# Attention of two heads on 64 rows of TensorE each, and the first gating units of batch 0 among the pairs of batch 1

## The chip, the cores and the metric

The program runs on one core of a Trainium2 chip. The metric is the device time of one execution in microseconds (us), lower is better. The kernel before took 448.5 us (median of three runs, 447.94 to 448.64). Beside these runs one execution was recorded by the hardware profiler: its own time is 448.29 us, and its trace spans 446.5 us from the first to the last instruction.

The engines that matter: TensorE (PE in the profile, with its weight loads as PEld), VectorE (DVE), ScalarE (ACT), GpSimd (POOL), and SyncE (SP), which issues the DMAs. Each works through its own instructions in order.

## The reference

```python
# attention: 2 batches, 12 heads, 448 positions, 64 dimensions per head
scores = cap * tanh((q @ k.T / 8) / cap)
attn = exp(scores - max); attn = attn / (sum(attn) + 1e-9)
x = attn @ v                              # heads side by side: (2, 448, 768)
# gated block
h = gelu_tanh(x @ w_in)                   # 768 -> 1024, halves u and v of 512
v_n = (v - mean(v)) / sqrt(var(v) + 1e-6) * g_ln
v_s = w_sg @ v_n + b_sg                   # over the 448 positions
x = x + (u * v_s) @ w_out
# mixer
u = x + (relu(x.T @ w_tok1) @ w_tok2).T   # over positions, 448 -> 256 -> 448
out = u + relu(u @ w_ch1) @ w_ch2         # 768 -> 1536 -> 768
```

All arithmetic is in 32-bit floats. The weights (all but `w_sg`) arrive as 64-bit floats.

## The kernel before

Everything is kept in a product form that TensorE runs at one pass: a float `a` is split into `a(0)`, its rounding to the type `fp32r`, and `a(1)`, the rest, and a product is the sum of three, `a(0)b(0) + a(0)b(1) + a(1)b(0)` (`three`). So each tile that TensorE reads has a cast (`cast`, on ACT, DVE or POOL) and a subtraction (`rest`, on DVE or POOL). Only the product of the attention weights with v is done in plain fp32: its matmul counts as two records in the trace and four passes in time.

**Attention** goes by 12 pairs of heads, six per batch (`attention(n)`). The scores are computed transposed, keys on the 128 output rows, the 448 queries as columns. A head has only 64 dimensions, so the kernel fills the 128 rows of the array with a trick: the tile `K` holds a head's keys on one half of the rows and their rests on the other, and q is loaded twice, once for each half. One matmul then gives two of the products, and two matmuls (with the cast of q and with its rest) give one block of 128 keys. The 448 keys are three blocks of 128 and 64 left over; the left-over keys of both heads share one block of four matmuls. A pair so has 16 matmuls for scores (L270 `sc<-a,K`), 12 records in fp32 for the values (L592 `gm<-a,V`) and 4 matmuls for the left-over keys' values (L604 `gm<-a,R`). ACT takes tanh (L551) and exp (L559) of the scores, two blocks at a time (128x896) with one block (128x448) at the end. Columns of ones beside v give the sums; DVE transposes them (L622), adds the guard, takes reciprocals (L630, L631), spreads them (L636), multiplies (L646) and splits x (L359 or L358, L375).

**After attention**: three v units and then, after a unit for the positions left over from both batches, four u units per batch (`v_unit`: 18 matmuls of 512 columns; `u_unit`: 18 of 448; both with gelu on ACT, L745), then `sg_unit`, `out_unit`, `tr_unit`, `tok1_unit`, `tok2_unit`, `ch1_unit`, `ch2_unit`.

**Weights** (`weight`) are turned from 64-bit to 32-bit on the chip: three ACT instructions (L405, L414, L427) and one of DVE (L434), and then split.

**Order.** Nothing loops: all operations are collected with a key (a due time) and `Plan.schedule` puts them in order by assumed durations, choosing among allowed engines (`ON`, `W_ON`) and giving out buffers from pools (`BUFS`). `gm` has four PSUM banks and `sc` two double ones. The order on each engine is then fixed in the program. Which weights are due when stands in `KEYS`. In the kernel before, the batches' units stand in the order

```python
        for b in range(B):
            vn[b] = stage([lambda s=s: self.v_unit(x[b], win_v, s) for s in range(NR)], 4)
...
        for b in range(B):
            u[b] = stage([lambda f=f: self.u_unit(x[b], win_u, f) for f in range(NF)], 3.4)
```

with keys that all lie after the last pair.

## Time and profile before

| | us |
|---|---|
| median of three runs | 448.5 |
| the profiled execution | 448.29 |
| its span | 446.5 |
| PE busy in the span | 426.6 (96%) |
| PEld busy | 363.9 (82%) |
| DVE busy | 295.0 (66%) |
| ACT busy | 254.8 (57%) |
| POOL busy | 116.6 (26%) |

A share is an average over two very different parts: the attention, to about 124 us, and all that follows. [...]

### The profile page before, as it was taken

Reading aid. Unit: us, or ns where it says so; the run is one execution under the profiler, and the core shown is the slowest. Engines: PE = TensorE matmul, PEld = TensorE weight load, DVE = VectorE, ACT = ScalarE, POOL = GpSimd, SP = SyncE. Lnnn points to the kernel's source line nnn. Section 1 sums busy time; section 2 is a strip of 40 time slices with the busy share of each in tenths; the row PEclk is TensorE's granted clock in tenths of the full one; section 3 lists DMA queues with packets and bytes.
Section 4 is the critical chain, followed back from the end, with each engine's and each line's share of the span. In section 5 each row is a group of like instructions: output and inputs, shape, how many; then the busy total and the mean of one; then the engine's idle time right before and its main releaser. Section 6 shows DMA issues by size and latency. Waiting matters only on the chain.

```text
span 446.5 us, 5466 instructions
## 1 busy us (share of the span) xinstructions
PE 426.6 (96%) x1966; PEld 363.9 (82%) x1966; DVE 295.0 (66%) x483; ACT 254.8 (57%) x380; POOL 116.6 (26%) x133
## 2 busy tenths in 40 slices
PE   8988999988999999999999999999999999999994
PEld 6655675655578899999999988999999999999994
DVE  5999999999998893787337899545454332434220
ACT  6969999988767656632226770755455523444100
POOL 2334566633213440176000177000002010111000
PEclk9999999999999999999999999999999999999998
DMA  7932443522123524402001312433344314452101
GB/s 204 340 116 85 133 147 115 155 65 66 47 94 96 181 83 150 131 0 94 2 0 42 101 48 69 139 123 94 99 137 117 120 37 167 132 159 93 73 37 32
DMA packets 24627, 46.02 MB, mean 103 GB/s; under 512 B 11536, under 2 KB 14352, under 8 KB 24592
## 3 DMA queue, kind: packets, MB, share of 16 engines
q1 hardware_dynamic: 24448, 45.48, 33.0%
q8 instruction: 17, 0.28, 0.3%
q14 instruction: 18, 0.15, 0.1%
q10 hardware_dynamic: 144, 0.11, 0.1%
HBM read 42.83 MB, written 2.75 MB: 102 GB/s over the span
## 4 chain that ended last, share of the span: by engine, by line
PE 70%; DVE 25%; issue 2%; SPq 1%; DMA 1%; DVEq 0%
PE gm L270 48%; PE sc L270 19%; DVE a L375 5%; DVE x L375 4%; DVE h L646 3%; DVE h L622 3%; DVE K L375 2%; DVE h L636 2%; DVE R L359 1%; DVE t L434 1%; PE sc L882 1%; DVE K L359 1%; DVE sm L630 1%; PE gm L592 1%; DVE x L359 1%
## 5 line engine op out<-in xcount | busy, mean ns | idle before, releaser
L270 PE MATMUL gm<-a,a 128*128 128x448 f32 (+1 forms) x824 | 166.8, 363 | 0.1
L270 PEld LDWEIGHTS gm<-a,a 128*128 128x128 f32 x824 | 153.1, 188 | 11.6 <-DVE h L949 0.5
L270 PE MATMUL sc<-x,a 128*128 128x448 f32 x432 | 88.2, 366 | 0.6 <-DVE x L375 0.6
L270 PEld LDWEIGHTS sc<-x,a 128*128 128x128 f32 x432 | 81.0, 188 | 7.7 <-DVE x L375 1.3
L434 DVE SCALAR_TENSOR_TENSOR t<-r,t 128x512 int32<-128x512 int32 (+1 forms) x58 | 42.3, 731 | 44.7 <-ACT t L427 43.4
L405 ACT ACTIVATE r<-r 128x512 f32<-128x512 f32 (+1 forms) x58 | 38.7, 666 | 40.9 <-DMA r<-ch_in 29.3
L414 ACT ACTIVATE t<-r 128x512 uint16<-128x512 uint16 (+1 forms) x58 | 45.4, 782 | 28.8 <-DVE a L375 28.8
L592 PE MATMUL gm<-a,V 128*128 128x448 f32 x144 | 59.3, 539 | 0.0
L868 POOL TENSOR_TENSOR h<-x 128x448 f32<-128x448 f32 (+1 forms) x25 | 34.9, 1421 | 75.9 <-DVE x L375 46.3
L270 PE MATMUL sc<-a,K 128*128 128x448 f32 x192 | 49.4, 394 | 1.5 <-DVE K L375 0.7
L363 POOL TENSOR_SCALAR a<-t 128x512 fp32r<-128x512 f32 (+1 forms) x21 | 13.6, 649 | 141.6 <-PE gm L270 70.4
L375 DVE TENSOR_TENSOR a<-t,a 128x512 fp32r<-128x512 f32 (+1 forms) x50 | 36.2, 726 | 20.6 <-POOL a L363 19.7
L551 ACT ACTIVATE a<-sc,qs 128x896 f32<-128x896 f32 (+1 forms) x48 | 42.0, 907 | 7.5 <-PE sc L270 7.3
L270 PEld LDWEIGHTS sc<-a,K 128*128 128x128 f32 x192 | 36.1, 191 | 10.9 <-issue 4.0
L427 ACT ACTIVATE t<-r 128x512 f16<-128x512 f32 (+1 forms) x58 | 44.7, 770 | 0.0
L559 ACT ACTIVATE a<-a,acap 128x896 f32<-128x896 f32 (+1 forms) x48 | 43.7, 943 | 0.1
L592 PEld LDWEIGHTS gm<-a,V 128*128 128x128 f32 x144 | 27.1, 189 | 16.4 <-issue 13.8
L375 DVE TENSOR_TENSOR a<-a,a 64x448 fp32r<-64x448 f32 (+2 forms) x37 | 29.5, 798 | 0.9
L270 PE MATMUL gm<-x,a 128*128 128x448 f32 x144 | 29.3, 365 | 0.0
L270 PEld LDWEIGHTS gm<-x,a 128*128 128x128 f32 x144 | 27.1, 188 | 2.2
L376 POOL TENSOR_TENSOR a<-t,a 128x512 fp32r<-128x512 f32 (+1 forms) x12 | 20.0, 1668 | 30.6 <-DVE a L359 18.5
L604 PE MATMUL gm<-a,R 128*128 128x448 f32 x48 | 17.7, 454 | 10.3 <-DVE a L375 10.2
(78 smaller groups left out, 393.8 us busy)
## 6 DMA issues: line engine op xcount, KB each, us to landing
r<-ch_in SPq DMA_DIRECT2D x36, 512.0 KB, 3.6
r<-w_in_in SPq DMA_DIRECT2D x12, 512.0 KB, 4.1
a<-q_in SPq DMA_DIRECT2D x11, 448.0 KB, 5.1
a<-k_in SPq DMA_DIRECT2D x11, 288.0 KB, 4.4
r<-w_out_in SPq DMA_DIRECT2D x6, 512.0 KB, 3.9
out_t<-h SPq DMA_DIRECT2D x11, 224.0 KB, 2.6
V<-v_in SPq DMA_DIRECT2D x24, 96.0 KB, 3.8
r<-tok_in SPq DMA_DIRECT2D x2, 512.0 KB, 3.7
```

The source lines that it names most:

```text
L270: self.nc.tensor.matmul(view(), l, rr, start=(i + m == 0), stop=(i + m == n - 1))
L375: "DVE": ("DVE", n / 0.96 + 68, lambda: nc.vector.tensor_tensor(**args()), not psum),
L376: "POOL": ("POOL", n * 2.3 + 60, lambda: nc.gpsimd.tensor_tensor(**args()), True),
L405: lambda: nc.scalar.activation(raw[:, :, 1].bitcast(F32), raw[:, :, 1].bitcast(F32), AF.Copy, scale=2.0**-112),
L414: lambda: nc.scalar.activation(t.ap.bitcast(U16)[:, 0::2], raw.ap.rearrange("p n t -> p (n t)").bitcast(U16)[:, 1::4], AF.Copy, scale=2.0* ...
L427: lambda: nc.scalar.activation(t.ap.bitcast(F16)[:, 1::2], raw[:, :, 1].bitcast(F32), AF.Copy),
L434: lambda: nc.vector.scalar_tensor_tensor(out=t.ap, in0=raw[:, :, 1], scalar=3, in1=t.ap, op0=ALU.logical_shift_left, op1=ALU.bitwise_or),
L551: lambda te=te, sc=sc, nn=nn: nc.scalar.activation(te.ap, sc[:, 0:nn, :S], AF.Tanh, scale=self.qs),
L559: lambda te=te: nc.scalar.activation(te.ap, te.ap, AF.Exp, scale=self.acap),
L592: nc.tensor.matmul(ps[:, :S], V[:, 3 * j + h : 3 * j + h + 2].rearrange("p c d -> p (c d)"), te[:, m, :], start=(j == 0), stop=False,)
L604: nc.tensor.matmul(ps[:, :S], R[:, 3 * i + h : 3 * i + h + 2].rearrange("p c d -> p (c d)"), T[:, h], start=False, stop=(i == 1),)
L868: lambda: self.nc.gpsimd.tensor_tensor(out=out.ap, in0=parts(0), in1=parts(1), op=ALU.add),
```

## The change

- q and k of a pair, and v of the left-over keys, come in one load of 128 x 1088 (`qk`, laid out so on the host), the lower 64 rows for one head and the upper 64 for the other. One cast and one subtraction split it, where there were separate ones for q, for each half of K and for R. v comes with its ones in one load (`va`).
- Scores: for each block of 128 keys, three products for each head, each a matmul on 64 rows: 18 such matmuls per pair in place of 12 on 128 rows. The left-over block takes three matmuls on 128 rows (four before). The left-over keys' values take six matmuls on 64 rows (four on 128 before). The 64-row matmuls alternate between the lower and the upper rows, and between two PSUM banks.
- They stand in two bursts per pair: the first two blocks (12 matmuls), and the third block with the left-over values of the pair before (6 and 6). A pair's values are computed while the next pair's scores are.
- The tiles T take one cast and one subtraction of 128x448 in place of two of each on 64 rows.
- The three v units and four u units of batch 0 get keys from 72 on (`EARLY`), among the pairs of batch 1. Their weights' keys are earlier, and the weights of the v units are turned to 32 bits by one ACT and three DVE instructions in place of three and one.
- Buffer pools are cut anew (`v`, `q`; `a` 21, `h` 13), and the planner's assumed durations are changed.

```diff
+KJ = (0, 576, 704, 832)
+QC, RC = slice(128, 576), slice(960, 1088)
+QKW = 1088
+THREE = ((0, 0), (0, 1), (1, 0))
...
-    "QH": {"ACT": 0, "DVE": 150, "POOL": 0},
-    "QL": {"DVE": 150},
-    "KH": {"ACT": 0, "DVE": 0, "POOL": 0},
-    "KL": {"DVE": 0, "POOL": -150},
-    "V": {"DVE": 150},
-    "VL": {"DVE": -150, "POOL": 600},
+    "QK": {"ACT": 0, "DVE": 300, "POOL": 0},
+    "QKL": {"DVE": 0},
...
 KEYS = {
-    "win_v": (44, 10),
-    "win_u": (121, 4),
+    "win_v": (6, 8),
...
-BUFS = {"x": 12, "a": 27, "r": 2, "t": 3, "h": 15, "p": 6, "gm": 4, "sc": 2, "sm": 4}
-SLOT = 189.5
+BUFS = {"x": 12, "v": 3, "q": 6, "a": 21, "r": 2, "t": 3, "h": 13, "p": 6, "gm": 4, "sc": 2, "sm": 4}
+EARLY = 72.0
+HALVES = ("win_u", "wsg", "wout", "tok1", "tok2", "ch1", "ch2")
...
         self.big = c("big", [1, 1], I32)
-        for i in range(2):
-            self.K.append([held("h", at("h", f"K{i}{h}", [128, 512], F32R)) for h in range(2)])
-            self.V.append(held("a", at("a", f"V{i}", [128, 9, 64], F32)))
-            self.R.append(held("const", c(f"R{i}", [128, 6, 64], F32R)))
-            nc.gpsimd.memset(self.K[i][0].ap.bitcast(F32)[:, S:512], 0.0)
-            nc.gpsimd.memset(self.K[i][1].ap.bitcast(F32)[:, 0:64], 0.0)
...
-        out = self.w([rows, 2, n], F32R)
+        out = self.buf("q" if name in ("wsg", "tok2") else "a", [rows, 2, n], F32R)
...
+            if name in HALVES:
+
+                self.act(
...
+            else:
+                self.dve(
...
+                    lambda: nc.vector.tensor_scalar(
+                        t.ap, raw[:, :, 1], 0x0FFFFFFF, 3, ALU.bitwise_and, ALU.logical_shift_left
+                    ),
...
+                for half, scalar, op in ((1, -0x80000000, ALU.bitwise_and), (0, 29, ALU.logical_shift_right)):
+                    self.dve(
...
+                        lambda half=half, scalar=scalar, op=op: nc.vector.scalar_tensor_tensor(
+                            out=t.ap, in0=raw[:, :, half], scalar=scalar, in1=t.ap, op0=op, op1=ALU.bitwise_or
+                        ),
...
-    def attention(self, n):
+    def pair_in(self, n):
...
+        parts = [slice(0, KJ[1]), slice(KJ[1], QKW)] if n == 0 else [slice(0, QKW)]
...
+            raw, hi, lo = (self.buf("a" if n == 0 else "q", [128, size], t) for t in (F32, F32R, F32R))
...
+            self.cast(size, lambda hi=hi: hi.ap, lambda raw=raw: raw.ap, [raw], [hi], ks + m * 0.2, on)
+            self.rest(
...
+    def scores(self, qk, js, key, more=(), extra=0.0):
...
+        def fn():
+            for sc, j in zip(scs, js):
+                ks = slice(KJ[j], KJ[j] + 128)
+                for t, (k, q) in enumerate(THREE):
+                    for h, rows in enumerate((LO, UP)):
+                        nc.tensor.matmul(
+                            sc[:, h, :S], part(k, rows, ks), part(q, rows, QC), start=(t == 0), stop=(t == 2)
+                        )
+            for f, _, _ in more:
+                f()
+
+        self.pe(
...
+            fn,
...
+    def rest_of(self, qk, T, A):
+        part, tiles = qk[:2]
+
+        def fn():
+            for v, e in THREE:
+                for h, rows in enumerate((LO, UP)):
+                    self.nc.tensor.matmul(A[h][:, :S], part(v, rows, RC), T[e][rows], start=False, stop=False)
...
+    def values(self, qk, E, A, js, key):
+        nc = self.nc
+        V = qk[2]
+        for j in js:
+            for h in range(2):
+
+                def av(j=j, h=h):
                     nc.tensor.matmul(
-                        ps[:, :S],
+                        A[h][:, :S],
                         V[:, 3 * j + h : 3 * j + h + 2].rearrange("p c d -> p (c d)"),
-                        te[:, m, :],
+                        E[j][:, h],
                         start=(j == 0),
-                        stop=False,
+                        stop=(j == 2),
                     )
-                self.pe(4, av, [V, te], [ps], kh)
...
-                for i in range(2):
-                    nc.tensor.matmul(
-                        ps[:, :S],
-                        R[:, 3 * i + h : 3 * i + h + 2].rearrange("p c d -> p (c d)"),
-                        T[:, h],
-                        start=False,
-                        stop=(i == 1),
...
-            self.pe(2, rest, [R, T], [ps], kh)
+                self.pe(3.7, av, [V, E[j]], [A[h]], key)
...
+    def attention_all(self):
+        nc = self.nc
+        xs = []
+        old = None
+        for n in range(B * NP + 1):
+            k0 = 10.0 * n
+            if n < B * NP:
+                qk = self.pair_in(n)
+                E = {j: self.a([128, 2, S]) for j in range(3)}
+                tr, TH, TL = self.h([128, 1, S]), self.h([128, S], F32R), self.h([128, S], F32R)
+                A = [self.bank() for _ in range(2)]
+                for js in ([[0], [1]] if n == 0 else [[0, 1]]):
+                    for i, (j, sc) in enumerate(zip(js, self.scores(qk, js, k0 + 0.3 * js[0]))):
+                        self.weigh(sc, 2, E[j], k0 + 0.1 * j)
+            if old:
+                oqk, oE, oT, oA = old
+                self.values(oqk, oE, oA, [0, 1], k0 + 0.5)
+                more = [self.rest_of(oqk, oT, oA)]
+            if n < B * NP:
+                (sc,) = self.scores(qk, [2], k0 + 4, more if old else ())
+                self.weigh(sc, 2, E[2], k0 + 4)
+                sc = self.bank2()
+
+                def last(sc=sc, part=qk[0]):
+
+                    ks, every = slice(KJ[3], KJ[3] + 128), slice(0, 128)
+                    for t, (k, q) in enumerate(THREE):
+                        nc.tensor.matmul(sc[:, 0, :S], part(k, every, ks), part(q, every, QC), start=(t == 0), stop=(t == 2))
+
+                self.pe(3.5, last, qk[1], [sc], k0 + 4.1)
+                self.weigh(sc, 1, tr, k0 + 4.1)
+                self.cast(S, lambda TH=TH: TH.ap, lambda tr=tr: tr[:, 0], [tr], [TH], k0 + 5, ON["TH"])
+                self.rest(
+                    S,
+                    lambda TL=TL: TL.ap,
+                    lambda tr=tr: tr[:, 0],
+                    lambda TH=TH: TH.ap,
+                    [tr, TH],
+                    [TL],
+                    k0 + 5,
+                    ON["TL"],
+                )
+            else:
+                f, r, w = more[0]
+                self.pe(3.5, f, r, w, k0 + 4)
+            if old:
+                self.values(oqk, oE, oA, [2], k0 + 5)
+                xs.append(self.normalise(n - 1, oA))
+            if n < B * NP:
+                old = qk, E, (TH, TL), A
+        return xs
...
-        attention = self.attention_anycap if self.anycap else self.attention
+        xs = [self.attention_anycap(n) for n in range(B * NP)] if self.anycap else self.attention_all()
...
-        for b in range(B):
-            vn[b] = stage([lambda s=s: self.v_unit(x[b], win_v, s) for s in range(NR)], 4)
+        early, k = (k, k - 70) if self.anycap else (k, EARLY)
+        vn[0] = stage([lambda s=s: self.v_unit(x[0], win_v, s) for s in range(NR)], 6.5)
+        u[0] = stage([lambda f=f: self.u_unit(x[0], win_u, f) for f in range(NF)], 6.5)
+        k = early
+        vn[1] = stage([lambda s=s: self.v_unit(x[1], win_v, s) for s in range(NR)], 4)
...
-        for b in range(B):
-            u[b] = stage([lambda f=f: self.u_unit(x[b], win_u, f) for f in range(NF)], 3.4)
+        u[1] = stage([lambda f=f: self.u_unit(x[1], win_u, f) for f in range(NF)], 3.4)
...
+    qk = np.zeros((B, NP, 2, 64, QKW), q.dtype)
+    va = np.ones((B, NP, 128, 9, 64), v.dtype)
+    qk[..., RC] = 1.0
+    for h in range(2):
+        kh = k.reshape(B, NP, 2, S, D)[:, :, h].transpose(0, 1, 3, 2)
+        for j in range(3):
+            qk[:, :, h, :, KJ[j] : KJ[j] + 128] = kh[..., j * 128 : (j + 1) * 128]
+            va[:, :, :, 3 * j + 2 * h] = vp[:, :, h, j * 128 : (j + 1) * 128]
+        qk[:, :, h, :, KJ[3] + 64 * h : KJ[3] + 64 * h + 64] = kh[..., REST]
+        qk[:, :, h, :, QC] = q.reshape(B, NP, 2, S, D)[:, :, h].transpose(0, 1, 3, 2)
+        qk[:, :, h, :, RC.start + 64 * h : RC.start + 64 * h + 64] = vp[:, :, h, REST]
...
```

**The order on TensorE, one pair.** Before, a pair's scores in the middle of the attention (n = 5; K_85 and K_86 are the keys' tiles of the two heads, a_397 and a_409 the cast and the rest of q, gm the sums with V):

```order
L270 MATMUL sc_537<-a_397,K_85 128x448
L270 MATMUL sc_537<-a_409,K_85 128x448
L270 MATMUL sc_537<-a_397,K_85 128x448
L270 MATMUL sc_537<-a_409,K_85 128x448
L270 MATMUL sc_546<-a_397,K_85 128x448
L270 MATMUL sc_546<-a_409,K_85 128x448
L270 MATMUL sc_546<-a_397,K_85 128x448
L270 MATMUL sc_546<-a_409,K_85 128x448
L270 MATMUL sc_546<-a_397,K_86 128x448
L270 MATMUL sc_546<-a_409,K_86 128x448
L604 MATMUL gm_518<-a_521,R_79 128x448 x2
L592 MATMUL gm_564<-a_523,V_78 128x448 x2
```

Now, at the same pair (q_441 and q_499 are the cast and the rest of the joint tile, v_318 is the v of the pair before, and x2 stands for the two heads' matmuls):

```order
L540 MATMUL sc_512<-q_441 128x448 x2
L540 MATMUL sc_512<-q_499,q_441 128x448 x2
L540 MATMUL sc_512<-q_441,q_499 128x448 x2
L540 MATMUL sc_513<-q_441 128x448 x2
L540 MATMUL sc_513<-q_499,q_441 128x448 x2
L540 MATMUL sc_513<-q_441,q_499 128x448 x2
L572 MATMUL gm_467<-a_454,v_318 128x448
L572 MATMUL gm_505<-a_454,v_318 128x448
L540 MATMUL sc_546<-q_441 128x448 x2
L540 MATMUL sc_546<-q_499,q_441 128x448 x2
L540 MATMUL sc_546<-q_441,q_499 128x448 x2
L561 MATMUL gm_467<-h_503,q_372 128x448
```

Two double banks of scores are now filled in one go; behind two fp32 matmuls of the pair before stands the second burst, the third block and then that pair's left-over values (L561). The left-over block of scores has moved behind it.

**The order on TensorE, the units of batch 0.** Before, behind the last pair's left-over values (R) come the v units of batch 0 (a_562 and so on are w_in, x_315 and so on the attention's results):

```order
L592 MATMUL gm_1121<-a_1110,V_87 128x448
L604 MATMUL gm_1121<-a_1101,R_88 128x448 x2
L270 MATMUL gm_1145<-a_562,x_315 128x512 x3
L270 MATMUL gm_1145<-a_646,x_372 128x512 x3
```

Now, between the values of pair 7 and the scores of pair 9:

```order
L572 MATMUL gm_882<-a_781,v_584 128x448
L572 MATMUL gm_891<-a_781,v_584 128x448
L274 MATMUL gm_937<-a_226,x_298 128x512 x3
L274 MATMUL gm_937<-a_303,x_394 128x512 x3
L274 MATMUL gm_937<-a_389,x_471 128x512 x3
L274 MATMUL gm_937<-a_445,x_574 128x512 x3
L274 MATMUL gm_937<-a_510,x_651 128x512 x3
L274 MATMUL gm_937<-a_615,x_767 128x512 x3
L540 MATMUL sc_983<-q_802 128x448 x2
L540 MATMUL sc_983<-q_928,q_802 128x448 x2
L540 MATMUL sc_983<-q_802,q_928 128x448 x2
```

The v unit of 18 matmuls stands inside the attention.

**The order on ACT.** Before, tanh (L551) and exp (L559) of pairs 10 and 11, with a weight's instructions among them:

```order
L551 ACTIVATE a_1021<-sc_1003,qs 128x896
L551 ACTIVATE a_1030<-sc_1013,qs 128x448
L559 ACTIVATE a_1021<-a_1021,acap 128x896
L559 ACTIVATE a_1030<-a_1030,acap 128x448
L551 ACTIVATE a_1051<-sc_1036,qs 128x896
L414 ACTIVATE t_1062<-r_906 128x512
L559 ACTIVATE a_1051<-a_1051,acap 128x896
```

Now, at pairs 8 and 9 (tanh is L514, exp L522, gelu L768):

```order
L522 ACTIVATE a_932<-a_932,acap 128x896
L522 ACTIVATE h_944<-h_944,acap 128x448
L350 CAST q_967<-q_923 128x1088
L768 ACT_TABLE_LOAD
L768 ACTIVATE h_1000<-gm_937 128x512
L396 ACTIVATE r_930<-r_930 128x512
L514 ACTIVATE a_1010<-sc_983,qs 128x896
L514 ACTIVATE a_1017<-sc_984,qs 128x896
L522 ACT_TABLE_LOAD
L522 ACTIVATE a_1010<-a_1010,acap 128x896
L522 ACTIVATE a_1017<-a_1017,acap 128x896
L350 CAST a_1035<-h_1000 128x512
```

A gelu has an ACT_TABLE_LOAD ahead of it, and the next exp has another. Seven units have 14 of them before the last exp of the attention.

## Rows read from the trace of the kernel before

**Rows 1.** Windows: busy us of each engine (count), granted clock, DMA share, GB/s.
```profile
4.90:124.30 119.40, 107.56 (x384) 71.47 (x385) 113.16 (x202) 105.62 (x139) 50.66 (x56) 1.00 0.44 133
124.30:441.10 316.80, 315.62 (x1569) 289.35 (x1567) 180.23 (x278) 147.10 (x239) 64.10 (x60) 1.00 0.30 92
```

**Rows 2.** The chain of waits, in order of time: start us, us, what.
```profile
14.84 2.25 PE gm L592 x6
...
123.12 0.63 DVE a L375
...
123.80 0.67 PE gm L604 x2
124.47 92.62 PE gm L270 x442
217.09 0.66 PE sc L882 x6
...
353.10 87.57 PE gm L270 x432
```

**Rows 3.** Timeline of PE, 100 to 160: start us, us, instruction, shapes, count.
```profile
124.31 24.66 PE L270 MATMUL gm<-a,x 128*128 128x512 f32 x108
148.81 4.24 PE L270 MATMUL gm<-a,p 128*128 128x512 f32 x18
```

**Rows 4.** Timeline of ACT, 59 to 72.
```profile
66.63 0.98 ACT L551 ACTIVATE a<-sc,qs 128x896 f32<-128x896 f32 x1
67.51 0.78 ACT L427 ACTIVATE t<-r 128x512 f16<-128x512 f32 x1
68.15 1.02 ACT L559 ACTIVATE a<-a,acap 128x896 f32<-128x896 f32 x1
69.07 0.62 ACT L551 ACTIVATE a<-sc,qs 128x448 f32<-128x448 f32 x1
69.59 0.67 ACT L405 ACTIVATE r<-r 128x512 f32<-128x512 f32 x1
70.14 0.67 ACT L559 ACTIVATE a<-a,acap 128x448 f32<-128x448 f32 x1
```

**Rows 5.** Timeline of ACT, 120 to 136.
```profile
124.63 0.77 ACT L427 ACTIVATE t<-r 128x512 f16<-128x512 f32 x1
125.42 1.28 ACT L745 ACT_TABLE_LOAD   x1
128.61 0.60 ACT L745 ACTIVATE h<-gm 128x512 f32<-128x512 f32 x1 [1.91 <-PE gm L270]
...
134.37 0.60 ACT L358 CAST a<-h 128x512 fp32r<-128x512 f32 x1
134.87 0.59 ACT L745 ACTIVATE h<-gm 128x512 f32<-128x512 f32 x1
```

**Rows 6.** Timeline of DVE, 28 to 70.
```profile
34.90 0.39 DVE L359 CAST x<-h 128x448 fp32r<-128x448 f32 x1
35.21 1.08 DVE L375 TENSOR_TENSOR a<-a,a 128x896 fp32r<-128x896 f32 x1
36.21 0.62 DVE L375 TENSOR_TENSOR x<-h,x 128x448 fp32r<-128x448 f32 x1
...
40.94 0.64 DVE L622 STREAM_TRANSPOSE h<-gm 64x448 f32<-64x448 f32 x1
...
48.12 0.65 DVE L434 SCALAR_TENSOR_TENSOR t<-r,t 128x512 int32<-128x512 int32 x1
```

**Rows 7.** Timeline of all engines, 0 to 14.
```profile
0.72 1.28 ACT L321 ACT_TABLE_LOAD   x1 [0.72 <-PEq L1139]
...
2.01 0.20 ACT L321 ACTIVATE guard<-mhalf 128x1 f32<-128x1 f32 x1
...
6.80 1.53 ACT L551 ACTIVATE a<-sc,qs 128x448 f32<-128x448 f32 x2
```

**Rows 8.** Groups by line and form: count, busy us, mean ns of one, idle before.
```profile
L270 PE MATMUL gm<-a,a 128*128 128x448 f32 x736 | 150.9, 366 | 0.1
```

331 lines of the change are left out of this document (126 added, 205 removed).

## The prediction

> **What bounds the kernel now.** I read the windows first, then the chain of waits, then the timelines of PE, ACT and DVE where the chain runs. The windows split the span at 124.3 us [rows 1]. Behind it PE is busy for 315.6 of 316.8 us: there the time is the number of matmuls times their price. Ahead of it DVE is busy for 113.2 of 119.4 us, ACT for 105.6 and PE for 107.6, and PE's is overstated, since a record lasts longer than a matmul costs. The chain says the same: through the attention it hangs almost wholly on DVE, its last piece there ends at 123.8, PE takes the last two matmuls of the left-over values, and then comes one unbroken run of 442 recorded matmuls [rows 2]. So the attention is bound by DVE, with ACT close behind, and all the rest by PE.
>
> Prices. A 448-column matmul costs 0.203 us (87.57 / 432 [rows 2]), a record in fp32 0.375 (2.25 / 6 [rows 2]), hence 0.75 per fp32 matmul, and a 512-column one 0.227 (from 124.31 to 148.81 for 108 [rows 3]). On ACT I take the distance between starts [rows 4, 5]: tanh of 896 0.88, exp of 896 0.92, tanh of 448 0.52, a weight's first instruction 0.55, its others 0.64, a cast of 512 0.50, gelu 0.5, and exp of 448 0.57 (its 0.67 less the 0.10 by which its neighbours overlap).
>
> **What goes away behind the attention.** Three v units are 54 matmuls at 0.227, 12.3 us; four u units 72 at 0.203, 14.6 us. Since PE has no idle time there, moving them out takes off all 26.9 us: from the attention's end to the end of the span 322.2 becomes 295.3. The units that stay, and everything after them, have the same matmuls in the same order. At the joint the new order has 30 matmuls of the remaining v units that need only earlier pairs, 6.8 us, which covers about 5 us in which DVE normalises the last pair (seven instructions of 0.65 [rows 6] and the short ones). I count the joint at nothing; without this cover it would cost up to those 5 us.
>
> **What the attention then holds, engine by engine.**
>
> PE: before, a pair needs 20 matmuls at 0.203 and six in fp32 at 0.75, 8.6 us, 103 us for twelve, so it had some 16 us of slack. Now a pair has 9 couples of 64-row matmuls for scores, 3 full ones, 3 couples for the left-over values and the same six in fp32. No row shows a 64-row matmul. The bounds are the price of one full matmul for a couple (0.203, both at once) and of two (0.406, one after the other). I take 0.203: the two work on disjoint rows and write to different banks, and the array already holds two matmuls at a time, for a record lasts 0.366 where they follow each other every 0.203 [rows 2, 8]. Then a pair needs 15 x 0.203 + 4.5 = 7.5 us, twelve 90.5, and with the moved units 117.4. For each change between full and half rows the array may have to run empty, between nothing and 0.366 - 0.203 = 0.16 us; 25 bursts with two changes each give 0 to 8 us, and I take the middle, 4. PE: 121 us.
>
> The Trainium skill ("TensorE: Matmul & The Clock Gate", LDWEIGHTS) speaks against a part of this: a weight load takes its time by columns, not by rows, about 107 ns for 128 columns, so that two half loads cost as much as two whole ones. Rows 2 have a bound: six transposes of 128 columns, each with its own load, take 0.66 us, 0.11 each with the load. By the page a couple would cost 0.214 if its loads stood one behind the other under the running matmul, 0.011 more, 1.6 us over 144 couples, all of it on PE.
>
> ACT: tanh and exp are as many as before: 36 x 0.88 + 36 x 0.92 + 12 x 0.52 + 12 x 0.57 = 77.9. Weights up to the last exp: 15 first instructions and 14 others (the v units' weights now leave two of three to DVE), 8.3 + 9.0 = 17.3. Casts: 6 of 448, 3 of 1088, 3 of 512 and 4 short ones, 8.7 by width. Seven gelus 3.5. That is 107.4, about what ACT does now. New are 14 table loads, two for each gelu, since the next exp needs its table back. A load lasts 1.28, and the instruction ahead of it held ACT for 0.79 instead of 0.64 [rows 5, 4], so 1.43 each, 20.0 us. ACT: 127.4 us.
>
> DVE: gone are the casts and subtractions of R, of K's halves, one half of T's and q's double width; new are the joint subtraction of 1088 columns (1.08 x 1088 / 896, 1.3 us, eleven times), 18 instructions more for the v units' weights and the three v units' statistics. By the new order up to the last x: 79 instructions of 448 columns at 0.65, 44 of 512 at about 0.68, 16 us for the joint subtractions, 12.6 for casts [rows 6], and 8 for the short ones, an estimate: 118 us, 5 more than now. POOL is at 51 of 119 us now [rows 1] and gets fewer instructions in this stretch, 33 in place of 56.
>
> So the three engines come close to each other, and ACT is the longest. It starts with the first tanh, at 6.8 now [rows 7]; with the first load's cast and subtraction each done in one piece I take 5.9. Behind the last exp come the left-over cast and subtraction, six 64-row matmuls and two in fp32, 3.7 us in all. ACT without a gap gives an end of the attention at 5.9 + 127.4 + 3.7 = 137.0; with the share that the busiest engine reaches now (113.2 / 119.4 = 0.948 [rows 1]) it gives 5.9 + 134.4 + 3.7 = 144.0. By halves the same comes out: up to the first gelu ACT has some 66 us of work, and from there PE has 65 (five pairs' worth and the units) against ACT's 61, so 5.9 + 68 + 65 and a few us of waits, about 141. I take 140.4.
>
> **Sum.** 140.4 + 295.3 = 435.7 us of span; with the 1.8 us around the span (448.29 - 446.5) 437.5. The profiled execution lies 0.2 us under the median of the runs, so nothing is added. The forecast's own range, by ACT's gaps and by PE's changes of rows, is 434 to 442.
>
> **Rivals.**
>
> *The 64-row matmuls run one after the other.* Then a pair has 27 in place of 15, and the attention needs on PE 12 x (27 x 0.203 + 4.5) + 26.9 = 146.7 us; from the first matmul at about 4.9 its end is at 151.6 without a wait and at 160 with the changes of rows: 449 to 457, slower, 453 in the middle. For it: no row shows two matmuls sharing the array by rows. Against it: the overlap of records above. PE overtakes ACT's 140.4 when a couple costs 0.30, and the time is that of before at 0.38; below 0.30 the price of a couple hardly matters. By the Trainium skill ("TensorEngine Tiling (Array Packing)", Key Properties) row tiles run loads and matmuls in parallel, which is against this rival, and a change of the mode drains the array, which I have as 4 us.
>
> *A change of ACT's table costs more than its record.* The engine may have to run empty and fill again. Rows bound it: from 1.43 to 3.3, which lies between the end of the work ahead of the second load of the trace and the gelu behind it [rows 5], most of which the trace puts down to PE. At the start the instruction behind the first load follows 0.01 after it [rows 7], against this rival. At 3.3 ACT has 153.6 us and the attention ends at about 163: 460. The time is that of before at 2.0 to 2.5 us per change. The Trainium skill ("ScalarE: Activation LUTs", What ACT_TABLE_LOAD costs) states 1.28 and a drain of 1.38, 2.66 together; by that ACT would need 144.6, the time 451 to 459, and rows 7 show the load but no such drain behind it.
>
> *The engines get in each other's way.* Three engines of 118 to 127 us, in fixed orders and through four and two PSUM buffers, wait for each other; at a share of 0.90 for ACT the attention ends at 151: 448, no change. Before, DVE reached 0.95 with the others at 0.88 to 0.90, so I expect less loss than that; 442 to 448 stands for part of it.
>
> *ACT finds less to do, or the planner's slack holds.* Without a gap 434, and 431 if ACT starts a little earlier and the joint gains.
>
> **How the numbers follow.** Forecast (434 to 442) 0.60; shorter 0.10; mutual waits (442 to 449) 0.13; 64-row matmuls in series (449 to 457) 0.11; dear table changes 0.06. About 0.2% is what a measurement of this kernel can tell from no change, 447.6 to 449.4. Faster takes the first two and 0.10 of the third: 0.80; same 0.04; slower 0.16. The range from 431 to 450 leaves out the dear tables, most of the series and little below.
>
> **What would show it.** In the changed kernel's trace: 64-row matmuls of a couple starting nearly together and couples 0.2 apart (right), or 0.2 between the two (the first rival); 14 table loads of 1.28 in the attention, with the next instruction at their end (right) or over 1 us later (the second); ACT busy for over 0.9 of the attention's stretch; the run of matmuls after the last pair beginning at about 140, with about 295 from there to the end. I am wrong if the attention ends past 150, or if the part behind it doesn't shrink by about 27 us because a weight or a statistic comes late.

## The result, and the profile after

The changed kernel takes 443.9 us (median of four runs, 443.56 to 444.37) against 448.6 of the kernel before (447.94 to 448.87): a ratio of 0.990, interval 0.988 to 0.992. Faster, as forecast, but by 4.7 us instead of 11, and 6.4 over the forecast time. The profiled execution took 444.1 us with a span of 442.3.

Read the new profile in the order of the prediction. The windows first, split where the units that stayed behind begin; columns as in rows 1.

```profile
5.90:144.20 138.30, 130.82 (x589) 80.68 (x589) 108.53 (x183) 131.74 (x169) 34.56 (x34) 0.99 0.40 132
144.20:437.10 292.90, 291.96 (x1444) 265.93 (x1442) 154.26 (x225) 132.03 (x214) 70.24 (x65) 1.00 0.26 86
...
13.00:78.30 65.30, 60.88 (x271) 34.90 (x272) 62.18 (x98) 60.54 (x83) 23.70 (x22) 0.97 0.49 162
78.30:140.50 62.20, 59.99 (x274) 40.81 (x273) 41.11 (x77) 60.69 (x73) 8.99 (x11) 1.00 0.26 82
```

Against [rows 1], the attention now ends at 144.2 instead of 124.3 (forecast 140.4), and from there to the end of the span there are 298.1 us instead of 322.2 (forecast 295.3). ACT is the busiest engine of the attention, 131.74 of 138.30 us, a share of 0.953. The two lower lines, from 13 us on, split it at the first gelu: ahead of it ACT is idle for 4.76 us and DVE is the busier of the two; behind it ACT is idle for 1.5.

The end of the chain of waits (start us, us, what), which answers to [rows 2]:

```profile
257.61 89.28 PE sc L274 x432
346.89 89.29 PE gm L274 x432
```

This is the first surprise. The same 432 matmuls of the last stage, ch2, in the same order, on tiles of the same shapes, take 89.29 us instead of 87.57: 206.7 ns each instead of 202.7. PE has no gap there in either kernel.

PE's timeline shows a burst, and the joint at the attention's end:

```profile
27.83 0.47 PE L540 MATMUL sc<-q 64*128 64x448 f32 x2
28.14 0.57 PE L540 MATMUL sc<-q,q 64*128 64x448 f32 x4
28.54 0.37 PE L540 MATMUL sc<-q 64*128 64x448 f32 x2
28.75 0.57 PE L540 MATMUL sc<-q,q 64*128 64x448 f32 x4
29.25 1.77 PE L572 MATMUL gm<-a,v 128*128 128x448 f32 x4
...
144.20 7.99 PE L274 MATMUL gm<-a,x 128*128 128x512 f32 x33
```

Twelve matmuls on 64 rows from 27.83 to 29.25, 1.42 us: six couples at about 0.20, with something more at the burst's two ends. So the rival of matmuls in series is out.

ACT's timeline at the first two table loads:

```profile
78.31 1.28 ACT L768 ACT_TABLE_LOAD   x1
79.61 0.60 ACT L768 ACTIVATE h<-gm 128x512 f32<-128x512 f32 x1
80.22 1.28 ACT L522 ACT_TABLE_LOAD   x1
81.52 0.67 ACT L522 ACTIVATE h<-h,acap 128x448 f32<-128x448 f32 x1
```

The gelu starts 0.02 behind the end of the load, the exp 0.02 behind the next one. All 14 loads last 1.283. So the rival of dear table changes is out too.

What ACT waited for most ahead of the first gelu (engine, line, waited for: us in total, times, longest), and then DVE's and POOL's timelines in the same stretch:

```profile
ACT a L514 <- PE sc L540: 2.0, 2, 1.1
ACT x L350 <- DVE h L616: 1.1, 1, 1.1
ACT q L350 <- DVE q L367: 1.1, 1, 1.1
```

```profile
25.52 2.36 DVE L367 TENSOR_TENSOR q<-q,q 128x1088 fp32r<-128x1088 f32 x1
...
37.23 1.28 DVE L367 TENSOR_TENSOR q<-q,q 128x1088 fp32r<-128x1088 f32 x1
...
40.38 0.43 DVE L351 CAST a<-t 128x512 fp32r<-128x512 f32 x1
...
46.84 1.37 DVE L351 CAST a<-t 128x512 fp32r<-128x512 f32 x1
```

```profile
25.14 1.59 POOL L368 TENSOR_TENSOR a<-t,a 128x512 fp32r<-128x512 f32 x1 [3.18 <-DVE a L351]
...
46.44 1.48 POOL L368 TENSOR_TENSOR h<-h,h 128x448 fp32r<-128x448 f32 x1 [3.17 <-issue]
```

The same DVE instruction takes 1.28 or 2.36, the same cast 0.43 or 1.37. The long ones begin while POOL is in an instruction (25.14 to 26.73, 46.44 to 47.92) and end about as long after its end as they last alone. The Trainium skill ("SBUF — State Buffer", SBUF: two separate sides) says that an instruction of VectorE with two inputs in SBUF, or in a mode that uses two ports, and one of GpSimd hold a shared pair of ports in turns, each for the whole instruction, so that the other blocks. These rows agree, with 0.9 to 1.1 us lost each time.

### The profile page after: what moved, and what is told of

Read it like the earlier page. It is cut to its first block, busy times and chain, and to the rows that moved or that the text cites. A ratio compares the mean times of both kernels' runs of the same rounds, so it can differ in the third digit from the quotient of the medians.

```text
span 442.3 us, 5467 instructions
## 1 busy us (share of the span) xinstructions
PE 427.0 (97%) x2050; PEld 350.2 (79%) x2050; DVE 264.8 (60%) x413; ACT 265.7 (60%) x386; POOL 105.5 (24%) x105
## 4 chain that ended last, share of the span: by engine, by line
PE 78%; ACT 12%; DVE 7%; issue 2%; POOL 0%; DVEq 0%; POOLq 0%; ACTq 0%
PE gm L274 48%; PE sc L274 20%; PE gm L572 5%; ACT a L514 3%; ACT a L522 3%; PE sc L540 2%; DVE t L449 1%; DVE q L367 1%; PE sc L905 1%; ACT L768 1%; DVE t L438 1%; DVE h L592 1%; PE gm L561 1%; PE sc L342 1%; DVE h L616 1%
## 5 line engine op out<-in xcount | busy, mean ns | idle before, releaser
L274 PE MATMUL gm<-a,a 128*128 128x448 f32 (+1 forms) x556 | 115.2, 363 | 0.0
L274 PEld LDWEIGHTS gm<-a,a 128*128 128x128 f32 x556 | 102.8, 188 | 8.4
L572 PE MATMUL gm<-a,v 128*128 128x448 f32 x144 | 61.8, 558 | 4.8 <-ACT a L522 2.8
L274 PE MATMUL gm<-q,a 128*128 128x448 f32 x268 | 57.3, 367 | 0.0
L274 PEld LDWEIGHTS gm<-q,a 128*128 128x128 f32 x268 | 50.3, 188 | 4.7
L572 PEld LDWEIGHTS gm<-a,v 128*128 128x128 f32 x144 | 25.5, 191 | 29.6 <-issue 20.6
L368 POOL TENSOR_TENSOR a<-t,a 128x512 fp32r<-128x512 f32 x21 | 29.4, 1402 | 77.6 <-DVE a L351 73.7
L367 DVE TENSOR_TENSOR a<-t,a 128x512 fp32r<-128x512 f32 x35 | 24.6, 704 | 20.7 <-POOL a L355 20.1
L522 ACT ACTIVATE a<-a,acap 128x896 f32<-128x896 f32 x36 | 36.5, 1043 | 0.1
L514 ACT ACTIVATE a<-sc,qs 128x896 f32<-128x896 f32 x36 | 35.1, 1004 | 2.2 <-PE sc L540 2.2
```

Of the source, the lines that this page charges most:

```text
L274: self.nc.tensor.matmul(view(), l, rr, start=(i + m == 0), stop=(i + m == n - 1))
L367: "DVE": ("DVE", n / 0.96 + 155, lambda: nc.vector.tensor_tensor(**args()), not psum),
L368: "POOL": ("POOL", n * 2.3 + 60, lambda: nc.gpsimd.tensor_tensor(**args()), True),
L514: lambda: nc.scalar.activation(te.ap, sc[:, 0:nn, :S], AF.Tanh, scale=self.qs),
L522: lambda: nc.scalar.activation(te.ap, te.ap, AF.Exp, scale=self.acap),
L572: nc.tensor.matmul(A[h][:, :S], V[:, 3 * j + h : 3 * j + h + 2].rearrange("p c d -> p (c d)"), E[j][:, h], start=(j == 0), stop=(j == 2),)
```

## The experiments

Fifteen kernels ran. PE's "end of attention" is the start of the 512-column matmuls of the remaining v units; "ch1, ch2" is what 432 matmuls of each took in the profiled execution; in the kernel before, ch1's 88.7 holds 1.1 of stops. e13's 119.0 comes from an execution that took 443.4, 2 us over its median.

| kernel | median us | ratio to before, interval | end of attention | ch1, ch2 |
|---|---|---|---|---|
| before | 448.6 | | 124.3 | 88.7, 87.6 |
| changed | 443.9 | 0.990 (0.988 to 0.992) | 144.2 | 89.3, 89.3 |
| e1 pause | 440.3 | 0.980 (0.977 to 0.983) | 143.3 | 87.8, 87.6 |
| e2 turn | 444.9 | 0.989 (0.985 to 0.993) | 144.2 | 89.3, 89.3 |
| e3 no tables | 439.2 | 0.978 (0.974 to 0.982) | 138.3 | 89.3, 89.3 |
| e4 attention alone | 443.8 | 0.989 (0.984 to 0.993) | 116.6 | 89.3, 89.3 |
| e5 by head | 444.1 | 0.991 (0.989 to 0.994) | 144.0 | 89.3, 89.3 |
| e6 decode on ACT | 448.5 | 1.000 (0.998 to 1.002) | 147.5 | 89.3, 89.3 |
| e7 no POOL | 442.0 | 0.986 (0.984 to 0.988) | 141.6 | 89.3, 89.3 |
| e8 tanh gelu, pause | 439.0 | 0.979 (0.977 to 0.981) | 142.5 | 87.8, 87.6 |
| e9 one matmul in a burst | 443.8 | 0.991 (0.987 to 0.994) | 143.6 | 89.3, 89.3 |
| e10 same rows | 465.0 | 1.039 (1.034 to 1.044) | 162.3 | 89.3, 89.3 |
| e11 no POOL, pause | 438.8 | 0.979 (0.976 to 0.981) | 141.9 | 87.8, 87.6 |
| e12 e11 with tanh gelu | 439.2 | 0.980 (0.977 to 0.982) | 142.5 | 87.8, 87.6 |
| e13 alone, pause | 441.4 | 0.984 (0.982 to 0.985) | 119.0 | 87.8, 87.6 |
| e14 alone, no POOL, pause | 444.2 | 0.991 (0.989 to 0.993) | 120.5 | 87.8, 87.6 |
| e15 v units only, no POOL, pause | 440.2 | 0.982 (0.980 to 0.983) | 128.5 | 87.8, 87.6 |

**Why do ch1 and ch2 go slower?** In the kernel before, PE stood still at 261 us (the next matmul began 0.48 after one, instead of 0.20). In that stage the matmuls follow each other at 206.7 ns up to the stop and at 202.7 behind it. PE stood still again at 270 to 272 us, in ch1, for DVE's subtractions. Its chain:

```profile
261.71 2.71 PE gm L270 x12
...
267.56 4.57 DVE x L375 x3
272.17 80.93 PE sc L270 x398
```

In the changed kernel no such stop is left. Theory: there are two steady paces, and what breaks the row sets which. e1 adds one column copied on ACT ahead of ch1:

```
+ nc.scalar.copy(ps_ch1[:, 0, 0:1], ps_of_last_tok2[:, 0:1])   # before the first matmul of ch1
```

> The changed kernel with one column of ScalarE's work more: before the first matmul of ch1, ScalarE copies one column of the last tok2 bank into the bank of ch1, so TensorE has to stand still there once, for about 0.5 us (TensorE's end to ScalarE's start, 0.2 of copy, and back). Every other instruction stands where it stood. Theory of two paces: in the changed kernel the 864 matmuls of ch1 and ch2 follow each other at 206.7 ns, in the kernel before at 202.7, where a stop of 0.48 us stood ahead of them; the stop puts the pace back: 864 x 4.0 ns = 3.4 gained, 0.5 paid: 441.0 (440.5 to 441.5), and 202.7 in the trace. Rival, the pace hangs on the tiles and their addresses, not on what went before: 206.7 stays, and the pause is paid: 444.4.

The chain of e1 (start us, us, what):

```profile
256.77 0.15 ACT sc L995
...
256.97 87.82 PE sc L275 x432
344.79 87.56 PE gm L275 x432
```

The first matmul starts 0.60 behind the last one, 0.40 more than in a row, and both stages run at the pace of before: 440.3, 3.6 faster, a little more than the theory's 441.0. In the two traces 2.7 of it lie behind the attention (295.4 us against 298.1); the other 0.9 lie ahead of the attention's end and are the clock's (last section). The last column of the table is the stronger evidence: all seven kernels with this pause have the faster pace, and all nine without it, the changed kernel among them, the slower. All seven have the same pause; a shorter one was not tried.

e2 puts six transposes in that place instead of a wait, because such blocks go along with changes of the pace earlier in both traces.

```
+ for i in range(6): nc.tensor.transpose(ps_ch1[...], ident, ident)
```

> The changed kernel with six transposes of 128 columns more, of no use, right before the first matmul of ch1 (0.65 us of TensorE), and no wait. In both traces the pace of the 448-column matmuls changes at blocks of six such transposes (206.7, then 202.7, then 206.7 again at 211, 214 and 217 us of the changed kernel). Theory of two paces that any break in the row of equal matmuls can change, without a stop: ch1 and ch2 at 202.7, 443.9 - 3.4 + 0.65 = 441.1. Rival, only a stop brings the faster pace: 206.7 stays, 443.9 + 0.65 = 444.5.

The chain of e2:

```profile
257.42 0.66 PE sc L995 x6
258.07 89.28 PE sc L275 x432
```

The slower pace stays and the transposes are paid, 444.9: here the stop brought the pace back and the break without a stop did not. What the two paces are in the hardware, no run tells, nor why blocks of transposes do go along with a change at 211 to 217 us.

**What are the tables worth, and what comes behind them?**

```
- AF.Gelu_apprx_tanh                                    # in gelu()
+ AF.Tanh if self.key < 118 else AF.Gelu_apprx_tanh     # batch 0's seven units
```

> The changed kernel with Tanh in place of Gelu in the seven v and u units of batch 0 (these units' values are left out so), which takes the 14 table loads out of ScalarE's attention, 14 x 1.283 = 18.0 us, and leaves every other instruction in its place. Theory, ScalarE is what bounds the second half of attention: its end falls from 144.2 until TensorE bounds, whose attention is 121 us from a start near 9.5: 131 to 134, and the time to 431 to 434. Rival, the first half (VectorE) and the banks set the end as much: not more than 4 us come off, 440 to 443.

A window of e3, from 70 us to the attention's end:

```profile
70.00:138.34 68.34, 68.34 (x316) 47.14 (x317) 50.04 (x94) 53.24 (x74) 10.59 (x13) 1.00 0.29 93
```

Of 18.0 us of loads only 5.9 come off the attention's end (4.7 off the time). From 70 us on PE has no gap: 138.3 is its floor, not the 131 to 134 that I expected. The time, 439.2, lies between the two expectations: the loads do count, but PE's own end lies only 6 us ahead of ACT's. So it went with e8, where the gelu is computed by Square, Tanh and three passes of DVE instead:

> The changed kernel with the pause before ch1 and with the gelu of the seven units of batch 0 computed without another table: Square on ScalarE, two passes of VectorE, Tanh on ScalarE, a third pass of VectorE (twice the gelu; the factor is taken into the epsilon of the statistics and into the product with u). ScalarE loses 14 loads (18.0) and gets seven passes (3), VectorE gets 21 passes (11). Without the tables alone the attention ended at 138.3 and 4.7 us came off, and with the pause alone 3.6. Theory: both hold, less what VectorE's passes cost, 0 to 3: 435.6 to 438.6. Rival, the five steps hold the two banks so long that TensorE waits for them, or VectorE becomes the bound: 440 or more.

439.0 is 1.3 under e1, between what the two theories gave: DVE's passes take back most of the gain (it is busy for 19.50 of 20 us from 70 to 90 in e8, 16.18 in the changed kernel).

**Do two 64-row matmuls share the array, and what does a change of rows cost?** e5 issues each block of six by head instead of in turns, e10 puts both heads on the lower rows, and e9 puts one full matmul between the two blocks of a burst.

```
- for t, (k, q) in enumerate(THREE):
-     for h, rows in enumerate((LO, UP)):
+ for h, rows in enumerate((LO, UP)):          # e5
+     for t, (k, q) in enumerate(THREE):

+     for h, rows in enumerate((LO, LO)):      # e10, order as in the changed kernel

+ if j == 1 and len(js) == 2:                  # e9, ahead of the second block
+     nc.tensor.matmul(sc[:, 0, :S], part(0, slice(0, 128), ks), part(0, slice(0, 128), QC), start=True, stop=True)
```

> The changed kernel with the matmuls on 64 rows ordered by head instead of in turns: per block of six, three on the lower rows and then three on the upper, on the same tiles and into the same banks; the other engines' order stays. If two neighbours on different rows run beside each other (0.20 for two in the trace), only the third and the fourth of a block still do: 5 slots of 0.203 for 3, 0.41 more in each of 48 blocks, 19.5 us of TensorE in the attention, of which the waits of its first half can take up some 4: attention ends at 159 to 164 instead of 144.2, and the time is 459 to 464. Rival, that neighbours don't run beside each other and the 0.20 is a matter of how the records are modelled: within 1 us of 443.9.

> The changed kernel with all matmuls on 64 rows moved to the lower 64 rows (both heads' scores and left-over values are then the first head's), so that no two can run beside each other. Nothing else is changed. Ordering by head cost nothing (444.1), either because two rows of neighbours run beside each other anyhow or because a 64-row matmul alone takes half of a full one. By the first, 6 matmuls take 1.22 instead of 0.61, 144 x 0.203 = 29 us of TensorE more, of which 4 to 10 fall into its idle time: 463 to 469. By the second: within 2 us of 443.9.

> The changed kernel with one matmul of 128 rows and 448 columns put into the middle of each of the eleven first bursts (pairs 1 to 11), between the two blocks of scores, into a bank that the next matmul overwrites; the order of all else stays. As a matmul it costs 0.203. Theory, a change between 64 and 128 rows empties the array: in the trace of the kernel without early tables the last couple is followed by a 128-row matmul after 0.49 instead of 0.20, and a 448-column matmul of 128 rows by a couple after 0.49 instead of 0.20, while the first couple takes 0.105 instead of 0.20: 0.89 a burst, 9.8 us of TensorE; its idle time in the first half takes up some of it: 448 to 453. Rival, as forecast (0.08 for each change, 0.16 at most): 0.37 to 0.53 a burst, 4 to 6 us, of which 2 to 4 are seen: 446 to 448.

PE's timelines, of e5, e10 and e9 in turn:

```profile
28.72 0.55 PE L540 MATMUL sc<-q 64*128 64x448 f32 x2
29.03 0.64 PE L540 MATMUL sc<-q,q 64*128 64x448 f32 x4
...
30.21 1.77 PE L572 MATMUL gm<-a,v 128*128 128x448 f32 x4
```

```profile
109.36 0.67 PE L540 MATMUL sc<-q 64*128 64x448 f32 x2
109.87 0.98 PE L540 MATMUL sc<-q,q 64*128 64x448 f32 x4
...
112.02 0.64 PE L572 MATMUL gm<-a,v 128*128 128x448 f32 x1
```

```profile
28.61 0.47 PE L544 MATMUL sc<-q 64*128 64x448 f32 x2
...
29.40 0.47 PE L539 MATMUL sc<-q 128*128 128x448 f32 x1
29.80 0.47 PE L544 MATMUL sc<-q 64*128 64x448 f32 x2
...
30.61 1.77 PE L576 MATMUL gm<-a,v 128*128 128x448 f32 x4
```

e5 missed its main expectation: the burst takes 1.49 instead of 1.42, and the time stays. The rows say how. The first product of the block (hi times hi, "q") stands twice in a row, then four of the mixed ones, though the program issues q; q,q; q,q of one head and then the same of the other. By these names matmuls on the upper rows start ahead of earlier ones on the lower rows; that the chip turned them round, and not the building of the program, the trace does not show. My rival had guessed "no change" too, but for a wrong reason, and e10 settles that: on the same rows matmuls follow each other every 0.21, a burst of twelve takes 2.66 us from 109.36, and the attention ends at 162.3. Two 64-row matmuls on different rows do run together, and had they not, the changed kernel would be 16 us slower than the one before (e10's four runs lie between 462 and 468).

In e9 the burst takes 2.00 us instead of 1.42: 0.58 for one matmul of 0.203, so 0.38 for two changes, 0.19 each. My own theory (0.69 for the two) and the forecast (0.08 each, at most 0.16) both miss it, on opposite sides; with 0.19 in place of 0.08 and some 50 changes PE's attention is about 5 us longer than forecast. The Trainium skill ("TensorEngine Tiling (Array Packing)", Key Properties) says that a change of the tiling mode drains the array; the 0.19 agrees. And yet e9's time, 443.8, is that of the changed kernel, below what either theory gave. PE had room for 11 such insertions, 6.4 us, in its idle time: while ACT and DVE set the attention's end, the changes of rows cost nothing.

**What bounds the first half?** e6 gives win_v's decoding back to ACT, e7 takes POOL out of the attention's casts and differences.

```
- HALVES = ("win_u", "wsg", "wout", "tok1", "tok2", "ch1", "ch2")
+ HALVES = ("win_v", "win_u", "wsg", "wout", "tok1", "tok2", "ch1", "ch2")   # e6

- "QK": {"ACT": 0, "DVE": 300, "POOL": 0},  "TH": {"ACT": 300, "POOL": 0},
- "TL": {"DVE": 0, "POOL": 0},  "XH": {"DVE": -150, "ACT": 150, "POOL": 300},
+ "QK": {"ACT": 0, "DVE": 300},  "TH": {"ACT": 300, "DVE": 0},               # e7
+ "TL": {"DVE": 0},  "XH": {"DVE": -150, "ACT": 150},
```

> The changed kernel with the six win_v weights decoded like all others: two passes more on ScalarE and two fewer on VectorE for each, in the attention's first 70 us. There VectorE is busy 9.8 of 10, ScalarE 8.8. Theory, VectorE bounds the first half: it gives up 6 x 1.1 to 1.8 = 7 to 11 us, ScalarE takes 6 x 0.8 = 5 into idle time of about 4.7; the end comes 2 to 4 us earlier: 440 to 442. Rival, that ScalarE is bound just behind: 444 to 447, ScalarE busy 9.9 of 10 from 13 us on.

> The changed kernel with GpSimd taken out of the casts and differences of the attention (qk, T and x); the planner gives them to VectorE and ScalarE. VectorE's fast casts and short operations took 1.2 to 1.4 instead of 0.21 to 0.43 where GpSimd worked beside them. Theory, GpSimd takes from VectorE as much as it does for it: VectorE's busy time in the first 144 us stays within 3 us though it has some 30 instructions more, and the time is 441 to 445. Rival, that GpSimd's work is a true relief: the attention gets longer by the work moved, 448 to 456.

e6 loses all that the change gained, 448.5, more than its rival had. A window of it:

```profile
30.00:50.00 20.00, 19.09 (x94) 11.06 (x93) 19.30 (x34) 20.00 (x28) 10.61 (x10) 1.00 0.62 207
```

ACT is full from 13 us on. So giving those weights to DVE, a small part of the change, is worth 4.6 us, and ACT stands right behind DVE in the first half. e7 gains 1.9, within its theory's range. The casts of decoded weights in the groups by line and form (count, busy us, mean ns of one, idle before), of the changed kernel and of e7:

```profile
L351 DVE CAST a<-t 128x512 fp32r<-128x512 f32 x29 | 17.5, 606 | 0.4
```

```profile
L351 DVE CAST a<-t 128x512 fp32r<-128x512 f32 x29 | 13.8, 477 | 0.3
```

The same 29 casts take 3.7 us less. POOL's busy time in the first 150 us falls from 36.05 to 14.42 while DVE's stays (116.08 and 117.40), though DVE does more instructions: for a good part of what POOL did for the attention, DVE paid in blocked time.

But the gain of 1.9 does not come from the first half. Windows up to the last exp of the seventh pair, of the changed kernel and of e7, and ACT's timeline of e7 at its first gelus:

```profile
5.90:66.51 60.61, 55.83 (x249) 30.77 (x250) 53.78 (x83) 56.91 (x78) 20.82 (x18) 0.97 0.53 178
```

```profile
5.90:68.42 62.52, 57.53 (x265) 31.82 (x265) 54.59 (x94) 61.02 (x79) 9.63 (x10) 1.00 0.55 184
```

```profile
80.17 1.28 ACT L768 ACT_TABLE_LOAD   x1
...
83.23 0.57 ACT L768 ACTIVATE h<-gm 128x512 f32<-128x512 f32 x1
...
87.31 1.28 ACT L522 ACT_TABLE_LOAD   x1
```

e7 is 1.9 us later there: ACT is idle for 1.5 us instead of 3.7, but it has 4.1 us more work, with four more casts of q. Behind that point e7 is 4.4 us shorter, and 2.6 of these are two table loads: the planner made a new order in which two gelus stand behind one load, so the attention has 12 loads instead of 14. In an attention without loads, leaving POOL out costs 2.8 (e14 444.2, e13 441.4, below). So the runs show POOL blocking DVE, but not that the kernel gains by leaving POOL out.

> The changed kernel without GpSimd in the attention's casts and differences, which alone gave 442.0, and with the pause before ch1, which alone took 3.6 off: if the two are independent, as two stages should be, 438.4 (437.5 to 439.3). Rival, that part of the 1.9 of the first was a chance of the run or of the pace: 439.5 to 440.5.

> The same with the gelu of batch 0's units by Square and Tanh besides (no table loads in the attention; 21 passes more of VectorE, 7 more of ScalarE). With GpSimd that took 1.3 off. Theory, TensorE is the floor of the second half (full from 70 us in the kernel without tables, end at 138.3): the attention ends at 137 to 139, 434.5 to 437. Rival, VectorE, which now has GpSimd's work and the gelu's, takes back what ScalarE gains: 438 to 440.

e11 comes to 438.8, 5.1 under the changed kernel and 2.1% under the kernel before; the two edits add up as expected. e12's theory fails (439.2), by its rival: from 70 to 90 us PE is busy for 18.97 of 20 us instead of e11's 20.00, and it waits for one of DVE's passes of the gelu:

```profile
PE gm L575 <- DVE h L781: 1.0, 2, 0.5
```

**What was moving the units worth?**

```
- vn[0] = stage([... v_unit(x[0], win_v, s) ...], 6.5)     # at EARLY
- u[0] = stage([... u_unit(x[0], win_u, f) ...], 6.5)
+ vn[0] = stage([... v_unit(x[0], win_v, s) ...], 4)       # e4, e13, e14: behind the attention, ahead of vn[1]
+ u[0] = stage([... u_unit(x[0], win_u, f) ...], 3.4)      # e4, e13, e14, e15: ahead of u[1]
```

> One part of the change alone: attention on 64 rows with its two bursts, buffers and decoding, but the v and u units of batch 0 behind the attention, as in the kernel before. ScalarE's attention loses 14 table loads (18.0) and seven gelus (3), TensorE's 26.9. Theory of the sum (ScalarE's work sets the end): attention ends at 144.2 - 21 = 123 instead of 144.2, behind it come 322 to 326: 446 to 451 with what lies around the span, so that moving the units was worth 2 to 7 and the 64 rows themselves next to nothing. Rival, the first half of attention already sets the end, whatever ScalarE does later: attention ends at 128 or later, 452 to 456, slower than the kernel before.

> Attention on 64 rows alone (the v and u units of batch 0 behind it, as before), with the pause before ch1. Alone it took 443.8, the changed kernel 443.9; with the pause the changed kernel took 440.3. Theory, moving the units is worth nothing, since the part of the attention in which they can run has as good as no idle time on TensorE: 440.2 (439.4 to 441). Rival, the two were equal by chance of the pace: more than 1 apart from 440.3 on either side.

> The same without GpSimd in the attention's casts and differences. With the units among the pairs that came to 438.8. Theory, GpSimd's share is worth about as much here, and moving the units nothing: 438 to 439.6. Rival, with the units behind the attention VectorE is at 9.7 of 10 from 30 to 90 us and has to take GpSimd's work too, so that the attention gets longer: 441 to 444, and moving the units is worth 2 to 5 here. Third, VectorE alone sets this attention and GpSimd holds it up more than it helps: 434 to 437, and moving the units is a loss.

> The changed kernel without GpSimd in the attention and with the pause (438.8), but with only the three v units of batch 0 among the pairs; its four u units stay behind the attention. 12.3 of the 26.9 us of TensorE and six of fourteen table loads move. Theory, units pay as long as they find idle time of TensorE, 3.7 us from 70 us on, and cost as much as they save after that: within 1 of 438.8. Rival, every unit costs the attention its two loads and its matmuls and none pays: between the kernel without any (the run above) and 438.8. If it is under 437.5, the best number lies between none and seven.

PE in e4, its last stretch and its joint:

```profile
70.00:116.60 46.60, 42.87 (x193) 23.63 (x192) 43.17 (x75) 42.72 (x57) 15.74 (x16) 1.00 0.40 122
...
116.61 25.04 PE L274 MATMUL gm<-a,x 128*128 128x512 f32 x108
```

Without the move the attention ends at 116.6, with it at 144.2: 27.6 us more ahead of the joint for 26.9 fewer behind it, and the times are the same (443.8, 443.9). The window says why. Batch 0's units can't run before about 70 us, since they need its six pairs, and from there PE is idle for only 3.7 us by its records (somewhat more by what matmuls cost, as a record is longer): moving 26.9 us of PE's work could save little more than that. At the faster pace the move is worth 1.1 (e13 441.4, e1 440.3), without POOL 5.4 (e14 444.2, e11 438.8), and half of the units lies between (e15 440.2, as its rival said). So e4's theory of the sum was 6 us too long for the attention and its rival wrong. e13's theory misses by 0.4 and its rival, more than 1 apart, just holds; but e13's executions differ by 2.8, and the three at a granted clock of 0.996 took 440.6 to 441.1, so the move is hardly worth more than that. Of e14's three the second came nearest, a little past its ranges: without POOL the first half is 2.0 longer here too (68.6 against e4's 66.6 to the seventh pair's last exp), and no loads fall away to make up for it.

## Why the prediction was wrong in size

Its direction, its 64-row matmuls and its table loads held. It is 6.4 us short, and two terms make up that and no more: 3.8 at the attention's end, 2.8 behind it (the profiled execution lies 0.2 over the median).

*The attention's end, 140.4 forecast, 144.2 measured.* I had worked out two ends, 137.0 with ACT without a gap and 144.0 with the share that the busiest engine had before, and took the middle. The measured share is 0.953 and the end is that of the second. The size of ACT's work held: to the end of the last exp (140.88) it is busy for 128.7 us, with 127.4 forecast, 14 loads of 1.283 among them, and the tail behind is 3.3, with 3.7 forecast. What failed is the step that halved the gap. Its check "by halves" had ACT come to the first gelu at 5.9 + 68 = 73.9; it came at 78.3, and from there to the end it took 65.9 as forecast (65 and some waits). The loss, 4.4 from 73.9 to 78.3, is all in the first half: ACT had 67.6 us of work there instead of some 66, and was idle for 4.8 where the check allowed 2. Of that idle time 2.2 is two waits for DVE, whose instructions take up to 1.1 us longer beside POOL, 0.9 is the clock's (last section), and the rest is waits for other scores and a load. What POOL's blocking cost the kernel stays open: without POOL ACT's idle time shrinks, but its work grows by more (e7). I had counted POOL's fewer instructions as no concern, and had a rival of mutual waits without saying between whom. The trace of before had shown the blocking; a cast of K, of half the rows, that took 0.39 at other times:

```profile
85.98 1.36 DVE L359 CAST K<-a 64x448 fp32r<-64x448 f32 x1
```

*PE in the attention, 121 forecast.* Low by about 5 for the changes of rows (0.19 against 0.08), by e9. It changed nothing here, as ACT was behind it, but it is why e3 ended at 138.3.

*Behind the attention, 295.3 forecast, 298.1 measured.* The step was "the units that stay, and everything after them, have the same matmuls in the same order", at 0.203 each. The count held and the price did not: 864 x 4.0 ns = 3.5. Against it stand the 1.1 us of stops in ch1 that the kernel before had, so that ch1 and ch2 together are 2.3 longer; the other 0.5 lies ahead of ch1 and at the end of the span. I took the price from one stage of the kernel before as a property of the shape. It was a property of the shape and of a stop at 261 us, of 0.48 from start to start, that the new order did away with. With the pause, e11's part behind its attention is 437.0 - 141.9 = 295.1.

*The joint* was costed at nothing, and rightly: in the changed kernel the first 512-column matmul follows the last pair without a wait.

*Rivals.* Matmuls in series: refuted (e10 shows what it would have been). The forecast held there, but its ground, that records overlap, could not carry it: in e10, where nothing runs together, records of 0.365 start every 0.207 and overlap as much. Dear table changes: refuted, next instruction 0.02 behind the load. Mutual waits: true in kind, 6.3 us of ACT's idle time up to the last exp, mostly ahead of the first gelu. What the prediction never asked is what the move was worth beside the rest of the change; it added up both on one attention and could not see that nearly all of the gain, 124.3 to 116.6, came with the attention's new form (e4). Which part of that form gave it, beside the decoding (e6), was not tried.

## What to carry to other kernels

Before moving work into a stage for its idle time, ask in which part of the stage the work can run, and count the idle time of that part: here 3.7 us, not 16. The pitch of a long run of equal matmuls is to be measured in the new kernel and not carried over; if it is some per cent above that of another stage or version, a single short wait ahead of the run is a cheap test: here it cost 0.5 us and bought 3.5. And the longest and the shortest of one VectorE instruction show whether GpSimd blocks it, but not what GpSimd's share is worth: where a planner makes a new order for the test, compare the orders, here the table loads, before the gain is put down to the edit.

## What the runs showed of the hardware

- Two steady paces of 448-column matmuls, each with its own weight load: 202.7 and 206.7 ns, one or the other for hundreds of matmuls, in every execution that was profiled. A stop of 0.6 us from start to start led to the faster one in all seven kernels that had it; a block of six transposes led to a change at 211 to 217 us and to none at 257.
- By the names in the trace, matmuls on different halves of the rows start out of program order: with three of one head issued ahead of three of the other, both heads' still start in turns, and the block takes no longer (1.49 against 1.42 us for two).
- The clock after the same short idle time differs from execution to execution. Two windows of the changed kernel's profiled execution, and the same of e1's:

```profile
60.00:62.00 2.00, 0.58 (x4) 0.21 (x3) 1.94 (x4) 2.00 (x3) 1.13 (x1) 1.00 0.00 0
...
64.00:66.00 2.00, 2.00 (x9) 1.26 (x8) 0.71 (x2) 2.00 (x4) 0.43 (x1) 0.50 0.21 80
```

```profile
60.00:62.00 2.00, 0.71 (x3) 0.32 (x3) 1.96 (x3) 2.00 (x4) 1.14 (x1) 1.00 0.01 4
...
64.00:66.00 2.00, 2.00 (x10) 1.05 (x7) 1.88 (x3) 2.00 (x4) 0.67 (x1) 1.00 0.82 189
```

PE does little in 60 to 62 in both; in the one the granted clock is then 0.50 of 2.4 GHz, the lower level of 1.2, in the other 1.00 (in e4, with 0.59 us of PE in 60 to 62, 1.00 too). In the first ACT waits 1.08 us for scores at 69.1, which it doesn't in the second, and comes to its first gelu 0.9 us later (78.31, 77.38).
